# A fused linear attention and gated MLP on one core: a list scheduler that counts on longer hand-overs, and two quads of keys projected in plain float32

## The chip, the core and the metric

The kernel runs on one core of a Trainium2 chip. The core has TensorE (PE: matmuls, 128 x 128, results in PSUM), VectorE (DVE), ScalarE (ACT), GpSimd (POOL) and SyncE (SP), which here only issues DMAs. Each engine works through its own queue strictly in order and waits where an input is not there. The metric is the device time of one execution in microseconds, as a median over runs.

## The reference

Two stages. First linear attention over 8 batches x 8 heads, 576 positions, head dimension 64, with 128 features:

```python
def phi(x):
    proj = np.einsum('bhsd,df->bhsf', x, w_phi)
    proj = proj - np.max(np.abs(proj), axis=-1, keepdims=True)
    return np.concatenate([np.exp(proj), np.exp(-proj)], axis=-1)
q_p, k_p = (phi(q), phi(k))
kv = np.einsum('bhsf,bhsd->bhfd', k_p, v)
z = np.sum(k_p, axis=2)
num = np.einsum('bhsf,bhfd->bhsd', q_p, kv)
den = np.einsum('bhsf,bhf->bhs', q_p, z)[..., None] + 1e-06
return (num / den).astype(np.float32)
```

Then, with the heads side by side as `x` (576 x 512 per batch), a gated MLP with 1024 hidden columns:

```python
h = np.maximum(x @ w_in, 0.0)
# conv_out: each column of h filtered along the sequence with 3 taps, conv_w
gate = 1.0 / (1.0 + np.exp(-conv_out))
return (h * gate @ w_out).astype(np.float32)
```

`w_in`, `conv_w` and `w_out` come as float64, the rest as float32.

## The kernel before

**Number formats.** Most matmuls are done in three passes of a faster float32 format (F32R): an operand is split into a rounded part (`hi`) and the rest (`lo`), and hi x hi, hi x lo and lo x hi are summed in PSUM. The rounding is one instruction (`round_op`, line 264, 267 or 270 by engine), the rest another (`rest_op`, line 276). Plain float32 operands (F32) need no split; the matmul is then one instruction, which the profile records as two.

**Attention.** Heads are taken four at a time, a *quad*; there are 16, two per batch. A quad's 576 positions are cut into five groups, one of 128 columns (g = 0) and four of 256. The names in the trace carry batch, quad and group: `kp3_1_2` is the key projection of batch 3, quad 1, group 2. For a key group (`k_group`): DMA into `kr`; POOL splits it into `kxh` (line 267) and `kxl` (276); TensorE projects it to `kp` in PSUM (lines 409 to 411); VectorE takes the maximum `km` (420) and subtracts it, `ks` (423); ScalarE makes two exponentials `ke` (443); TensorE multiplies them with the values into `kv` (452, 456). For a query group (`q_group`), one quad later: `qr`, `qxh`, `qxl`, `qp`, `qm`, `qs` in the same way, then TensorE transposes `qs` into `tp` (506), ScalarE makes `qe` (521) and rounds it to `qh` (264), VectorE makes the rest `ql` (276), and TensorE multiplies with `kv` into `nm` (539, 546). The queries of the first two quads (`NQ_F32`) are projected in F32 from `qr` directly (line 406). Numerators are copied to `num` (587), denominators to `dr` (580) and by DMA to `den`; VectorE inverts them (`rc`), four DMAs spread them into the single buffer `rr`, and the matmul `rb` (613) copies them over the partitions; VectorE multiplies to `xf` (616), which is split into `xh` and `xl`.

**MLP.** Each batch has two halves of 288 columns, n = 0 to 15. For each, eight blocks f: `hp` (640) is x times `w_in`, 12 matmuls; ScalarE's Relu gives `h` (651); POOL makes the middle tap of `c` (664), VectorE adds two taps (670). One sigmoid over all of `c` (675) follows, with ScalarE's function table changed before and after; then `c` times `h` (683), split into `gh` (264) and `gl` (276), and `op` (704) times `w_out` into `os` (712), which a DMA stores.

**Weights.** The 16 blocks of `w_in` and `w_out` are brought from float64 to hi and lo on the chip during the first 200 us: four VectorE, three ScalarE and two POOL instructions each (lines 314 to 329, `w_t`).

**What sets the order.** All instructions are collected as ops (`op`) with an engine, a planned duration, a rank (urgency) and their inputs. `Order.run` is a list scheduler: it walks through planned time and, on each free engine, takes the ready op of lowest rank. An op is ready when its inputs have ended in the plan and the hand-over between the engines (`LATENCY`, less `OVERLAP` on VectorE and ScalarE) has passed, and when its buffers' earlier users have ended and their `LATENCY` has passed. The plan's times are used for nothing else: what it leaves is the order on each engine. On the chip the queues run that order, each instruction waiting for its real inputs.

Of the kernel before, what the change touches and what calls it, by code (L numbers as in the profile page):

```python
# [23 lines left out]
NH = 11  # L24

NQ_F32 = 2
NKV_F32 = 2
LAG = 3.0

PE, DVE, ACT, POOL, SP = "PE", "DVE", "ACT", "POOL", "SP"  # L30


class Buf:
# [4 lines left out]
    def __init__(self, pool, shape, dtype, name, tag, bufs, seq=None):  # L38


        self.args = (pool, shape, dtype, name, tag, bufs)
        Buf.count += 1
        self.seq = Buf.count if seq is None else seq
        self.ring = (id(pool), tag)
        self.bufs = bufs
        self.ops = []
        self.state = {}
        self.tile = None
# [16 lines left out]
class Order:  # L65
# [1 line left out]

    LATENCY = {PE: 250, DVE: 180, ACT: 180, POOL: 150, SP: 0}  # L70
    OVERLAP = {PE: 0, DVE: 60, ACT: 60, POOL: 0}
    TABLE_NS = 1283

    def __init__(self):
        self.ops = []
# [43 lines left out]
    def run(self):  # L119
        free = {e: 0.0 for e in (PE, DVE, ACT, POOL, SP)}  # L120
        waiting = {e: [] for e in free}
        rings, alloced = {}, set()
        line = {}
        for b in {b for o in self.ops for b in o.bufs}:
            if b.seq != "any":
                line.setdefault(b.ring, []).append(b)
        for bs in line.values():
            bs.sort(key=lambda b: b.seq, reverse=True)
        table, dma = None, 0.0
        for o in self.ops:  # L130
            o.left, o.at = len(o.deps), 0.0
            o.end = None
            if not o.left:
                waiting[o.eng].append(o)
        done, now, order = 0, 0.0, []
        while done < len(self.ops):
            best = None
            nxt = []
            for e, ws in waiting.items():
                if free[e] > now:  # L140
                    nxt.append(free[e])
                    continue
                pick = None
                for o in ws:
                    if o.at > now:
                        nxt.append(o.at)
                        continue
                    if pick is not None and pick.rank <= o.rank:
                        continue
                    ok = True  # L150
                    for b in o.bufs:
                        if b in alloced:
                            continue
                        if b.seq != "any" and line[b.ring][-1] is not b:
                            ok = False
                            break
                        ring = rings.setdefault(b.ring, [])
                        if len(ring) >= b.bufs:
                            old = ring[-b.bufs].ops
                            if any(x.end is None for x in old):  # L160
                                ok = False
                                break
                            t = max(x.end + self.LATENCY[x.eng] for x in old)
                            if t > now:
                                nxt.append(t)
                                ok = False
                                break
                    if ok:
                        pick = o
                if pick is not None:  # L170
                    best = pick
                    break
            if best is None:
                nxt = [t for t in nxt if t > now]
                if not nxt:
                    raise RuntimeError("no order: " + ", ".join(
                        f"{o.eng} {[b.args[3] for b in o.bufs]}" for ws in waiting.values() for o in ws)[:1500])
                now = min(nxt)
                continue
            o = best  # L180
            waiting[o.eng].remove(o)
            for b in o.bufs:
                if b not in alloced:
                    alloced.add(b)
                    rings[b.ring].append(b)
                    if b.seq != "any":
                        line[b.ring].pop()
            o.start = now
            ns = o.ns
            if o.table is not None and o.table != table:  # L190
                ns += self.TABLE_NS
                table = o.table
            if o.eng == SP:

                free[SP] = now + 60
                dma = max(dma, now) + ns
                o.end = dma + 2000
            else:
                o.end = now + ns
                free[o.eng] = o.end - self.OVERLAP[o.eng]  # L200
            for u in o.users:
                u.left -= 1
                u.at = max(u.at, o.end + (0 if u.eng == o.eng != SP else self.LATENCY[o.eng] - self.OVERLAP.get(o.eng, 0)))
                if not u.left:
                    waiting[u.eng].append(u)
            order.append(o)
            done += 1
        return order
# [3 lines left out]
def kernel(  # L212
# [119 lines left out]
    def weight_split(src, n, rank, hi, lo, hi_b, lo_b):  # L332

        name = f"w{n}_"
        if src.dtype == F32:
            raw = sbuf([P, 512], F32, f"{name}r", "gh", 2)
            dma(rank - 2, 256, lambda: raw.t, lambda: src, w=[raw])
            round_op(POOL, rank, 512, hi, lambda: raw.t, [(hi_b, n)], [raw])
            rest_op(POOL, rank, 512, lo, lambda: raw.t, hi, [(lo_b, n)], [raw, (hi_b, n)])
            return  # L340
        raw = sbuf([P, 1024], I32, f"{name}r", "gh", 2)
        dma(rank - 2, 512, lambda: raw.t, lambda: src, w=[raw])
        tmp = sbuf([P, 2, 512], F32, f"{name}t", "gl", 2)
        float64_round(rank, 512, lambda: raw.t, lambda: tmp[:, 0, :], lambda: tmp[:, 1, :],
                      raw, (tmp, 0), (tmp, 1))
        round_op(ACT, rank, 512, hi, lambda: tmp[:, 0, :], [(hi_b, n)], [(tmp, 0)])
        rest_op(POOL, rank, 512, lo, lambda: tmp[:, 0, :], hi, [(lo_b, n)], [(tmp, 0), (hi_b, n)])
# [16 lines left out]
    def load_weight(n, rank):  # L364
        if n < 8:
            c, sl = n // 2, slice((n % 2) * 512, (n % 2) * 512 + 512)
            weight_split(w_in[n], n, rank, lambda: win_hi[c][:, sl], lambda: win_lo[c][:, sl], win_hi[c], win_lo[c])
        else:
            c = n - 8
            weight_split(w_out[c], n, rank, lambda: wout_hi[c].t, lambda: wout_lo[c].t, wout_hi[c], wout_lo[c])  # L370
# [5 lines left out]
    def group_columns(g):  # L376
        return (512, 1) if g == 0 else ((g - 1) * 256 + (P if g > 2 else 0), 2)

    def load_split(src, b, qd, g, kind, rank):
        c0, n = group_columns(g)  # L380
        ap = lambda: src[b, qd, :, c0 : c0 + n * P]
        if kind == "q" and 2 * b + qd < NQ_F32:
            raw = sbuf([P, n * P], F32, f"{kind}r{b}_{qd}_{g}", kind + "xh", 2)
            dma(rank - 3, 64 * n, lambda: raw.t, ap, w=[raw])
            return n, raw, None
        raw = sbuf([P, n * P], F32, f"{kind}r{b}_{qd}_{g}", kind + "r", 2)
        dma(rank - 3, 64 * n, lambda: raw.t, ap, w=[raw])
        hi = sbuf([P, n * P], F32R, f"{kind}xh{b}_{qd}_{g}", kind + "xh", 2)
        lo = sbuf([P, n * P], F32R, f"{kind}xl{b}_{qd}_{g}", kind + "xl", 2)
        round_op(POOL, rank, n * P, lambda: hi.t, lambda: raw.t, [hi], [raw])  # L390
        rest_op(POOL, rank, n * P, lambda: lo.t, lambda: raw.t, lambda: hi.t, [lo], [raw, hi])
        return n, hi, lo
# [75 lines left out]
    def kv_ready(u):  # L468
# [4 lines left out]
        for i in range(2):  # L473
            kf = None
            if u >= NKV_F32:
                kf = sbuf([P, 2, 2 * VW], F32, f"kvf{b}_{qd}_{i}", "kvf", 2)
            hi = sbuf([P, 2, 2 * VW], F32 if u < NKV_F32 else F32R, f"kvh{b}_{qd}_{i}", "kvh", 4)
            first = hi if kf is None else kf
# [15 lines left out]
    def q_group(j):  # L494
# [13 lines left out]
        op(PE, 110 * 2 * n, rank, turn, w=[tp], r=[pr, idn])  # L508
        f32 = u < NKV_F32 or g == 0
        qh = sbuf([P, 2, 2, n * P], F32 if f32 else F32R, f"qh{b}_{qd}_{g}", "qh", 2)  # L510
# [111 lines left out]
    def moe_rank(n):  # L622
        return 10.0 + LAG + 5.0 * n

# [89 lines left out]


    for n in range(16):
        load_weight(n, 1 + 0.9 * n)
    hs = {}
    for j in range(5 * NQ * B + 5):
        if j < 5 * NQ * B:  # L720
            k_group(j)
        if j >= 5:
# [3 lines left out]
            if (j - 5) % 10 == 9:  # L726
                b = (j - 5) // 10
# [66 lines left out]
```

## Time and profile before

| | |
|---|---|
| median of 3 runs | 930.44 us (924.73 to 931.77) |
| profiled execution | 931.45 us, of which its instructions span 929.7 us |
| granted TensorE clock in it, mean | 0.972 |
| TensorE busy in the first 200 us | 156.1 us |
| MLP block hp, first | at 121.8 us |
| last stretch, op of the last half batch | 900.7 to 926.3 us |

The profile names work by line, engine and tile. A wait is put down to the instruction whose end came last before the waiting one started. A matmul's record is longer than its share of a stream, since matmuls are pipelined: the next one starts before the record of the one ahead ends. The granted clock is the share of full speed that TensorE was given in a stretch.

### The profile page before, as it was taken

What the parts mean: (1) busy time and instruction counts of PE and PEld (TensorE: products, weight loads), DVE (VectorE), ACT (ScalarE), POOL (GpSimd) and SP (SyncE); (2) the same over time, 40 slices, a digit from 0 to 9 for tenths busy, and PEclk for the clock granted to TensorE, in tenths of its full rate; (3) what the DMA queues carried; (4) which work ended last, traced back from release to release, by engine and by line L of the source; (5) the groups of instructions that cost most, each with busy time, mean ns of one, the idle gap of its engine ahead of it and who ended that gap; (6) DMA issues with size and microseconds to landing.
All of it is one profiled execution on the core that took longest, in us unless ns stands there. A gap on an engine that the chain in (4) does not pass through costs nothing.

```text
span 929.7 us, 17861 instructions
## 1 busy us (share of the span) xinstructions
PE 820.5 (88%) x6414; PEld 789.4 (85%) x6414; DVE 640.9 (69%) x1294; ACT 573.1 (62%) x1230; POOL 305.7 (33%) x469
## 2 busy tenths in 40 slices
PE   6977589789999889988999879998899989998998
PEld 5866588689998879988899879998789988998998
DVE  5666888887668676767776667686776677675652
ACT  4575666667666576666766646576666647574432
POOL 4553656441423223332322313242142323211110
PEclk9797989899999999999999999999999999999999
DMA  6343331121111111111211111121112110000001
GB/s 191 114 121 89 94 96 36 30 54 55 42 48 54 43 44 46 55 35 45 59 43 49 41 44 45 41 60 33 52 48 60 36 42 25 20 20 21 21 15 50
DMA packets 56336, 49.19 MB, mean 53 GB/s; under 512 B 15028, under 2 KB 54200, under 8 KB 56248
## 3 DMA queue, kind: packets, MB, share of 16 engines
q1 hardware_dynamic: 56248, 48.05, 17.9%
q8 instruction: 51, 0.84, 0.4%
q14 instruction: 37, 0.30, 0.1%
HBM read 38.14 MB, written 9.44 MB: 51 GB/s over the span
## 4 chain that ended last, share of the span: by engine, by line
PE 43%; DVE 20%; ACT 13%; issue 10%; DMA 4%; POOL 2%; SPq 1%; POOLq 0%; ACTq 0%; DVEq 0%
PE op L704 12%; PE hp L640 8%; PE nm L546 6%; PE kv L456 6%; DMA rr<-rc 3%; DVE c L670 3%; PE tp L506 3%; DVE ql L276 3%; ACT qh L264 3%; PE nm L539 2%; ACT num L587 2%; DVE gl L276 2%; DVE ks L423 2%; PE kv L452 2%; ACT ke L443 2%
## 5 line engine op out<-in xcount | busy, mean ns | idle before, releaser
L670 DVE SCALAR_TENSOR_TENSOR c<-h,cw,c 128x288 f32<-128x288 f32 (+1 forms) x256 | 143.4, 572 | 46.9 <-POOL c L664 43.8
L640 PE MATMUL hp<-xh,win_hi 128*128 128x290 f32 x512 | 154.7, 302 | 9.3 <-ACT h L651 7.0
L456 PEld LDWEIGHTS kv<-v,ke 128*128 128x128 f32 x1024 | 156.8, 198 | 6.6 <-ACT ke L443 2.3
L456 PE MATMUL kv<-v,ke 128*128 128x65 f32 x1024 | 160.0, 257 | 2.0 <-ACT ke L443 1.9
L640 PE MATMUL hp<-xl,win_hi 128*128 128x290 f32 x512 | 153.3, 300 | 0.4 <-DVE xl L276 0.4
L640 PE MATMUL hp<-xh,win_lo 128*128 128x290 f32 x512 | 152.8, 298 | 0.0
L704 PE MATMUL op<-gh,wout_hi 128*128 128x288 f32 x512 | 152.1, 297 | 0.0
L704 PE MATMUL op<-gl,wout_hi 128*128 128x288 f32 x512 | 150.8, 295 | 0.0
L704 PE MATMUL op<-gh,wout_lo 128*128 128x288 f32 x512 | 150.6, 294 | 0.0
L664 POOL TENSOR_SCALAR c<-h,cw 128x288 f32<-128x288 f32 x128 | 76.2, 597 | 215.7 <-ACT h L651 185.2
L443 ACT ACTIVATE ke<-ks 128x512 f32<-128x512 f32 (+1 forms) x160 | 87.1, 580 | 66.7 <-DVE ks L423 66.1
L276 DVE TENSOR_TENSOR ql<-qe,qh 128x512 fp32r<-128x512 f32 x112 | 84.0, 760 | 64.0 <-ACT qh L264 63.3
L587 ACT ACTIVATE num<-nm 64x256 f32<-64x256 f32 (+1 forms) x192 | 61.8, 322 | 99.6 <-PE nm L546 54.9
L267 POOL TENSOR_SCALAR kxh<-kr 128x256 fp32r<-128x256 f32 (+1 forms) x80 | 39.7, 496 | 250.8 <-PE kp L410 240.4
L640 PEld LDWEIGHTS hp<-xh,win_hi 128*128 128x128 f32 x512 | 98.5, 192 | 12.5 <-ACT h L651 8.3
L640 PEld LDWEIGHTS hp<-xl,win_hi 128*128 128x128 f32 x512 | 98.1, 192 | 0.6 <-DVE xl L276 0.6
L640 PEld LDWEIGHTS hp<-xh,win_lo 128*128 128x128 f32 x512 | 98.5, 192 | 0.0
L506 PE MATMUL tp<-idn,qs 128*128 128x128 f32 x288 | 48.2, 287 | 55.7 <-DVE qs L423 38.1
L704 PEld LDWEIGHTS op<-gh,wout_hi 128*128 128x128 f32 x512 | 96.4, 188 | 0.0
L704 PEld LDWEIGHTS op<-gh,wout_lo 128*128 128x128 f32 x512 | 96.4, 188 | 0.0
L704 PEld LDWEIGHTS op<-gl,wout_hi 128*128 128x128 f32 x512 | 96.4, 188 | 0.0
L506 PEld LDWEIGHTS tp<-idn,qs 128*128 128x128 f32 x288 | 32.7, 145 | 67.1 <-issue 31.4
(86 smaller groups left out, 2002.4 us busy)
## 6 DMA issues: line engine op xcount, KB each, us to landing
v<-in_vt_dram SPq DMA_DIRECT2D x80, 130.0 KB
out_dram<-os SPq DMA_DIRECT2D x64, 144.0 KB
kr<-in_kT_dram SPq DMA_DIRECT2D x64, 128.0 KB
qr<-in_qT_dram SPq DMA_DIRECT2D x64, 128.0 KB
w_r<-in_w_in_dram SPq DMA_DIRECT2D x8, 512.0 KB
w_r<-in_w_out_dram SPq DMA_DIRECT2D x8, 512.0 KB
rr<-rc SPq DMA_DIRECT2D x128, 2.2 KB
kr<-in_kT_dram SPq DMA_DIRECT2D x16, 64.0 KB
```

The source lines that it names most:

```text
L264: op(ACT, t_act(n), rank, lambda: nc.scalar.activation(out=hi(), in_=src(), func=AF.Copy), w=w, r=r)
L267: lambda: nc.gpsimd.tensor_scalar(out=hi(), in0=src(), scalar1=1.0, scalar2=0.0, op0=ALU.mult, op1=ALU.add),
L276: lambda: e.tensor_tensor(out=lo(), in0=src(), in1=hi().bitcast(F32), op=ALU.subtract), w=w, r=r)
L443: op(ACT, t_act(256 * n), rank, lambda s=s: nc.scalar.activation(out=e[:, s], in_=pr.t, func=AF.Exp, scale=1.0 - 2.0 * s), w=[(e, s)], r=[ ...
L456: nc.tensor.matmul(out=kp[i][:, s, p0 : p0 + VW], lhsT=lhsT, rhs=v[:, (2 * t + i) * VW : (2 * t + i + 1) * VW], start=False, stop=(g % 2 = ...
L506: nc.tensor.transpose(out=tp[:, i, t, :], in_=pr[:, 2 * t + i, :], identity=idn.t)
L546: nc.tensor.matmul(out=ps[:, i, o : o + w], lhsT=w_, rhs=x_, start=(k == 0), stop=(k == 5))
L587: op(ACT, 170 + 0.82 * w, rank, lambda i=i, o=o, w=w, s0=s0, nt=nt: nc.scalar.activation(out=nt[D * i : D * i + D, s0 : s0 + w], in_=ps[0: ...
L640: nc.tensor.matmul(out=ps.t, lhsT=w_, rhs=x_, start=(p == 0 and k == 0), stop=(p == 3 and k == 2))
L664: op(POOL, 620, rank, lambda f=f, hs=hs: nc.gpsimd.tensor_scalar(out=c4[:, f, :], in0=hs[:, o : o + TC], scalar1=cw3[:, f, 1:2], scalar2=0 ...
L670: op(DVE, 550, rank, lambda f=f, hs=hs, j=j, lo=lo, hi=hi: nc.vector.scalar_tensor_tensor(out=c4[:, f, lo:hi], in0=hs[:, o + j - 1 + lo : ...
L704: nc.tensor.matmul(out=ps.t, lhsT=w_, rhs=x_, start=(f == 0 and k == 0), stop=(f == 7 and k == 2))
```

## The change

Three things. The planner's hand-over times grow: from TensorE 250 to 560 ns, from VectorE and ScalarE 180 to 420, from POOL 150 to 400; the same numbers delay the reuse of buffers. A new table `SLACK` adds to each hand-over between two engines, for ops of rank above 0, 400 ns where the waiting engine is TensorE and 100 ns where it is VectorE, ScalarE or POOL. And the keys of the first two quads (`NK_F32`, batch 0) are projected in F32: no `kxh` and `kxl` on POOL for those ten groups, one F32 matmul per tile in place of three. Their raw tiles then use the buffers of `kxh`. The two names for the weights' ranks keep their values.

```diff
+NK_F32 = 2
+W_RANK, W_STEP = 1.0, 0.9
...
-    LATENCY = {PE: 250, DVE: 180, ACT: 180, POOL: 150, SP: 0}
+    LATENCY = {PE: 560, DVE: 420, ACT: 420, POOL: 400, SP: 0}
     OVERLAP = {PE: 0, DVE: 60, ACT: 60, POOL: 0}
     TABLE_NS = 1283
+
+    SLACK = {PE: 400, DVE: 100, ACT: 100, POOL: 100, SP: 0}
...
-                u.at = max(u.at, o.end + (0 if u.eng == o.eng != SP else self.LATENCY[o.eng] - self.OVERLAP.get(o.eng, 0)))
+                gap = 0 if u.eng == o.eng != SP else self.LATENCY[o.eng] - self.OVERLAP.get(o.eng, 0)
+                if u.eng != o.eng and u.rank > 0:
+                    gap += self.SLACK[u.eng]
+                u.at = max(u.at, o.end + gap)
...
-        if kind == "q" and 2 * b + qd < NQ_F32:
+        if 2 * b + qd < (NQ_F32 if kind == "q" else NK_F32):
...
-        load_weight(n, 1 + 0.9 * n)
+        load_weight(n, W_RANK + W_STEP * n)
```

The order changes on every engine. Line numbers of the changed kernel are 7 higher from the planner's loop on. The numbers at the end of names count buffers.

VectorE at the query group of batch 3, quad 0, group 1, from its maximum `qm` on, before:

```order
L420 TENSOR_REDUCE qm3_0_1_4049<-qp3_0_1_3896 128x4
L616 TENSOR_TENSOR xf2_3_0_4059<-num2_1_1_3339,rb2_3_0_4047 128x290
L616 TENSOR_TENSOR xf2_3_1_4067<-num2_1_1_3339,rb2_3_1_4051 128x290
L423 TENSOR_TENSOR ks3_1_1_4071<-kp3_1_1_3886,km3_1_1_4044 128x512
L276 TENSOR_TENSOR xl2_3_0_4083<-xf2_3_0_4059,xh2_3_0_4069 128x290
L276 TENSOR_TENSOR gl3_0_4086<-c3_3471,gh3_0_4073 128x288
L276 TENSOR_TENSOR xl2_3_1_4093<-xf2_3_1_4067,xh2_3_1_4081 128x290
L276 TENSOR_TENSOR gl3_0_4086<-c3_3471,gh3_0_4073 128x288 x3
L276 TENSOR_TENSOR gl3_4_4124<-c3_3471,gh3_4_4107 128x288 x4
L423 TENSOR_TENSOR qs3_0_1_4133<-qp3_0_1_3896,qm3_0_1_4049 128x512
```

and after:

```order
L427 TENSOR_REDUCE qm3_0_1_3985<-qp3_0_1_3818 128x4
L283 TENSOR_TENSOR xl2_2_0_3991<-xf2_2_0_3948,xh2_2_0_3973 128x290
L283 TENSOR_TENSOR xl2_2_1_3999<-xf2_2_1_3970,xh2_2_1_3987 128x290
L430 TENSOR_TENSOR qs3_0_1_4003<-qp3_0_1_3818,qm3_0_1_3985 128x512
L427 TENSOR_REDUCE km3_1_2_4015<-kp3_1_2_3950 128x4
```

The subtraction `qs`, for which TensorE's `tp` waits, stands ahead of the eight `gl` and not behind them.

VectorE where the second quad's first group comes, batch 3, quad 1, group 0, with one step of the convolution `c`, before:

```order
L420 TENSOR_REDUCE km4_0_0_4549<-kp4_0_0_4529 128x2
L420 TENSOR_REDUCE qm3_1_0_4552<-qp3_1_0_4535 128x2
L423 TENSOR_TENSOR ks4_0_0_4560<-kp4_0_0_4529,km4_0_0_4549 128x256
L670 SCALAR_TENSOR_TENSOR c4_4163<-h4_6_4533,cw_77,c4_4163 128x287
L423 TENSOR_TENSOR qs3_1_0_4578<-qp3_1_0_4535,qm3_1_0_4552 128x256
```

and after:

```order
L427 TENSOR_REDUCE km4_0_0_4473<-kp4_0_0_4451 128x2
L427 TENSOR_REDUCE qm3_1_0_4475<-qp3_1_0_4456 128x2
L430 TENSOR_TENSOR ks4_0_0_4485<-kp4_0_0_4451,km4_0_0_4473 128x256
L430 TENSOR_TENSOR qs3_1_0_4488<-qp3_1_0_4456,qm3_1_0_4475 128x256
L677 SCALAR_TENSOR_TENSOR c4_4160<-h4_6_4468,cw_77,c4_4160 128x287
```

`c` moved behind `qs`.

TensorE in the first 200 us, from the projection `qp0_1_0` to its transposes `tp0_1_0`, before:

```order
L406 MATMUL qp0_1_0_658<-wbd_f_70,qr0_1_0_514 128x256
L409 MATMUL kp1_0_1_666<-wbd_hi_71,kxh1_0_1_603 128x256
L410 MATMUL kp1_0_1_666<-wbd_lo_72,kxh1_0_1_603 128x256
L411 MATMUL kp1_0_1_666<-wbd_hi_71,kxl1_0_1_608 128x256
L409 MATMUL kp1_0_1_666<-wbd_hi_71,kxh1_0_1_603 128x256
L410 MATMUL kp1_0_1_666<-wbd_lo_72,kxh1_0_1_603 128x256
L411 MATMUL kp1_0_1_666<-wbd_hi_71,kxl1_0_1_608 128x256
L506 MATMUL tp0_1_0_703<-idn_73,qs0_1_0_696 128x128 x2
```

and after, the last rows before the transposes (`qp0_1_0` itself stands 16 rows ahead of them):

```order
L418 MATMUL kp1_0_1_557<-wbd_hi_71,kxl1_0_1_503 128x256
L546 MATMUL nm0_0_3_568<-qh0_0_3_496,kvh0_0_0_318 65x256
L463 MATMUL kv0_1_0_373<-v0_1_3_320,ke0_1_3_461 128x65 x2
L546 MATMUL nm0_0_3_568<-qh0_0_3_496,kvh0_0_0_318 65x256
L463 MATMUL kv0_1_1_378<-v0_1_3_320,ke0_1_3_461 128x65 x2
L546 MATMUL nm0_0_3_568<-qh0_0_3_496,kvh0_0_1_324 65x256
L463 MATMUL kv0_1_0_373<-v0_1_3_320,ke0_1_3_461 128x65 x2
L546 MATMUL nm0_0_3_568<-qh0_0_3_496,kvh0_0_1_324 65x256
L463 MATMUL kv0_1_1_378<-v0_1_3_320,ke0_1_3_461 128x65 x2
L513 MATMUL tp0_1_0_599<-idn_73,qs0_1_0_566 128x128 x2
```

A whole group of `nm` with its share of `kv`, and a transpose of the group before (further up), moved in between `qp` and `tp`.

## The prediction

> **What bounds the kernel now.** I read the page's totals first, then TensorE's waits in two windows (the first 200 us and the rest), then single places in the timeline, then the table of stretches for the granted clock.
>
> ```profile
> PE 820.5 (88%) x6414; PEld 789.4 (85%) x6414; DVE 640.9 (69%) x1294; ACT 573.1 (62%) x1230; POOL 305.7 (33%) x469
> ```
>
> TensorE is the busiest engine. It has 12% idle, and no other engine is near full over the whole span. So what can be won without less work is TensorE's idle time, and the question is who ends it. First 200 us, then the rest (each row: who waited for whom, total us, times, longest):
>
> ```profile
> PE tp L506 <- DVE qs L423: 13.2, 8, 3.3
> PE hp L640 <- ACT h L651: 7.0, 2, 6.0
> PE tp L506 <- ACT w_t L316: 6.6, 1, 6.6
> PE kp L409 <- POOL kxh L267: 6.1, 4, 3.6
> ```
>
> ```profile
> PE tp L506 <- DVE qs L423: 24.9, 25, 1.8
> PE rb L613 <- DMA rr<-rc: 18.4, 14, 2.0
> PE tp L506 <- ACT ke L443: 8.2, 10, 1.2
> ```
>
> One place in the program dominates both: tp, the transposes of the projected queries, which need the subtraction qs on VectorE. After 200 us tp waits 24.9 + 8.2 = 33.1 us in 35 waits, 0.95 us each. That is a hand-over TensorE to VectorE and back inside one group: qp (TensorE), qm and qs (VectorE), tp (TensorE). The next row, rb waiting for the DMAs into rr, is a different chain.
>
> Is it the hand-over itself that is long, or VectorE's queue? Two waits of the steady part, in time order. First tp of the group (3,0,1):
>
> ```profile
> 329.38 3.41 DVE L276 TENSOR_TENSOR gl<-c,gh 128x288 fp32r<-128x288 f32 x7
> 332.71 0.68 DVE L423 TENSOR_TENSOR qs<-qp,qm 128x512 f32<-128x512 f32 x1
> ```
>
> ```profile
> 333.44 0.66 PE L506 MATMUL tp<-idn,qs 128*128 128x128 f32 x4 [1.72 <-DVE qs L423]
> ```
>
> qs ends at 333.39 and tp starts at 333.44: the hand-over takes 0.05 us. What came late is qs, which stands behind seven gl in VectorE's queue. Second, tp of (3,1,0):
>
> ```profile
> 362.11 0.28 PE L411 MATMUL qp<-wbd_hi,qxl 128*128 128x256 f32 x1
> 363.56 0.41 DVE L420 TENSOR_REDUCE km<-kp 128x2 f32<-128x256 f32 x1
> 364.55 1.05 DVE L670 SCALAR_TENSOR_TENSOR c<-h,cw,c 128x287 f32<-128x287 f32 x1
> 365.53 0.41 DVE L423 TENSOR_TENSOR qs<-qp,qm 128x256 f32<-128x256 f32 x1
> 366.08 0.41 PE L506 MATMUL tp<-idn,qs 128*128 128x128 f32 x2 [1.17 <-DVE qs L423]
> ```
>
> The last qp ends at 362.39, qs at 365.94. VectorE gets to the group's km 1.17 us after qp's end, and a convolution step c (1.05 us here) stands between. So the planner's old 0.12 us from VectorE to TensorE is about what the chip takes; the loss is that nothing is left over when VectorE runs late. The change gives just such a reserve.
>
> **The change part by part.** *Longer hand-overs and slack, steady part.* The planner now lets tp start 0.76 us after qs (0.12 before) and qm 0.66 us after qp (0.25 before). It does not slow the chip; it moves other TensorE work in between. I counted the TensorE work that stands in the order between a group's last qp and its tp. It costs this much per matmul of 288 columns (54 of them in 7.18 us, 0.133 each):
>
> ```profile
> 264.13 7.18 PE op L704 x54
> ```
>
> With 0.12 us for each kp and qp, the work in one batch (batch 3, the same in 4 to 6) is, before and after: first quad, groups 0 to 4: 2.6 to 3.8 us, 12.7 to 11.8, 3.1 to 7.4, 2.4 to 3.1, 2.4 to 4.0; second quad: 2.6 to 2.6, 7.2 to 8.7, 7.9 to 3.1, 1.9 to 4.1, 2.4 to 5.5. The seven classes that have 3.1 us or less before are those that wait, with (3,0,1). Six of the seven gain 0.7 to 4.3 us, against a mean wait of 0.95. The seventh, (b,1,0), gains no work, but the c of 1.05 us no longer stands between its ks and qs. The class (b,0,1) loses 0.9 us of work, but its qs now stands ahead of all eight gl, of which the seven above took 3.41 us. The class (b,1,2) falls to 3.1 us; VectorE needs 0.68 us each for qm and qs there, behind four gl, so it can wait up to about 1 us where it did not.
>
> What stays: 0.1 to 0.6 us in six or seven (b,1,0), 3.6 at most, and 1.5 for the newly short class; 5 in all. Bounds: everything goes (33.1) or, if VectorE's lateness grows with the reserve, nothing. I take 28 because in each class the added work is larger than the wait seen.
>
> *rb and rr.* Late next is this chain:
>
> ```profile
> 431.20 3.09 SPq L246 DMA_DIRECT2D rr<-rc  x4
> ...
> 435.51 0.51 PE L613 MATMUL rb<-rr,sel_r 128*128 128x290 f32 x2 [1.22 <-DMA rr<-rc]
> ```
>
> rr has one buffer. Its four DMAs are issued as soon as the pair of rb before has read it (SyncE needs 3.09 us for them), and the next rb starts 435.51 - 431.20 = 4.3 us after the first issue. In the order 24 op (3.2 us) stand between two pairs before; after, 24 op for one and 24 op with 6 kp (3.9 us) for the next. That saves 0.7 once a batch. But the pair ahead of them was covered by a tp wait that goes, and has 3.9 us of work against 4.3. I take 0 of the 18.4, with -5 to +8 as bounds (plus 8: twenty pairs at 1.3 each are 26).
>
> *The first 200 us.* Here tp has almost no cover: in the first four quads several tp stand 0.4 to 0.9 us behind their qp. One of them, (0,1,0):
>
> ```profile
> 60.18 0.65 PE L406 MATMUL qp<-wbd_f,qr 128*128 128x256 f32 x2
> ...
> 60.79 0.28 PE L410 MATMUL kp<-wbd_lo,kxh 128*128 128x256 f32 x1
> ...
> 62.93 0.41 PE L506 MATMUL tp<-idn,qs 128*128 128x128 f32 x2 [1.40 <-DVE qs L423]
> ```
>
> In the second quad the cover grows from 0.7, 0.9, 2.9, 0.9, 0.4 us to 4.0, 3.5, 4.8, 6.8, 3.9. tp waits 13.2 + 6.6 = 19.8 us here. But VectorE is nearly full once the weights and batch 1 run together (the stretch from 110 to 200 us below: 77.31 of 90), and what it has to do there is not less. So I take 14 of the 19.8: all that lies before 110 us but the 6.6, which ends on the weights' chain, and little after. Bounds 0 and 19.8.
>
> *The f32 keys.* POOL loses two instructions in each of ten groups:
>
> ```profile
> L276 POOL TENSOR_TENSOR kxl<-kr,kxh 128x256 fp32r<-128x256 f32 (+1 forms) x80 | 61.9, 774 | 5.7
> ...
> L267 POOL TENSOR_SCALAR kxh<-kr 128x256 fp32r<-128x256 f32 (+1 forms) x80 | 39.7, 496 | 250.8 <-PE kp L410 240.4 <-PE kv L456 5.4 <-DMA kr<-in_kT_dram 4.8
> ```
>
> That is 10 x (0.77 + 0.50) = 12.7 us of an engine that is a third busy. On the path only the wait kp <- kxh counts, 6.1 us with 3.6 of it the start of the program, when the data still lands. I take 2 (bounds 0 and 6.1). TensorE pays: from the start of the qp above to the second kp is 0.61 us, less 0.12 for the first kp is 0.49 for one f32 tile, against 3 x 0.12 = 0.36. That is +0.13 for 18 tiles, +2.3 us; bounds 0.2 (0.65 less a tail of 0.28) and 5.2 (0.65 without that deduction). The start lists keys of batch 1 ahead of a group of batch 0 in SyncE's queue, 0.2 MB more before it; it is inside the 2.
>
> *The granted clock.* Waits cost twice in the first part, as it seems:
>
> ```profile
> 34.00:40.00 6.00, 5.97 (x37) 5.51 (x36) 5.50 (x10) 2.43 (x6) 3.83 (x6) 0.68 0.27 80
> 50.00:60.00 10.00, 6.73 (x39) 5.75 (x37) 6.53 (x13) 5.38 (x11) 6.57 (x7) 0.83 0.32 94
> 80.00:90.00 10.00, 5.61 (x22) 4.81 (x23) 6.71 (x12) 4.72 (x10) 4.38 (x6) 0.61 0.41 115
> 110.00:120.00 10.00, 4.45 (x27) 4.42 (x28) 9.03 (x19) 4.46 (x9) 3.68 (x4) 0.66 0.25 80
> 110.00:200.00 90.00, 72.01 (x540) 68.74 (x541) 77.31 (x142) 57.72 (x123) 47.94 (x60) 0.91 0.19 54
> ```
>
> (Columns: TensorE, its weight loads, VectorE, ScalarE, POOL busy with counts, granted clock, DMA.) In the stretches that hold the long waits the clock is 0.83, 0.61 and 0.66; the share lost of the busy time is 6.73 x 0.17 + 5.61 x 0.39 + 4.45 x 0.34 = 4.8 us. If the low clock follows the waits, these go too; I leave them out of the sum and in the lower bound. The Trainium skill ("TensorE: Matmul & The Clock Gate", Part 1) says the clock halves after an idle window of about 3.4 us and is released after about 3.4 us of sustained work. By that rule only the waits of 6.6 us and 6.0 us would throttle, and the sum stays as it is; by the rows, where a longest wait of 3.3 us is followed by low clock, it would be 4.8 us lower. The row from 34 to 40 us speaks against the release too: TensorE is busy 5.97 of 6 us at 0.68.
>
> **Sum**, on the profiled execution (931.45 us, span 929.7): 931.45 - 28 - 0 - 14 - 2 + 2.3 = 889.8. That execution lies 1.0 above the median of the runs, so 889 against 930.44.
>
> **The rivals.**
> *Half of it turns into other waits.* TensorE reaches rb and nm earlier and waits there. For: rr's chain is a fixed 4.3 us; and the cover between tp and its nm in the second quad falls from 12.4 to 8.4 (group 1) and 9.8 to 6.7 us (group 4). Against: nm waits for nearly nothing now. Price: rb +7.6 (26 less 18.4), nm 1 us in seven batches, half the prologue's 14: 889 + 7.6 + 7 + 7 = 911.
> *The change does not do what it says.* VectorE's lateness (POOL ahead of c, contention) grows as the order moves, so the waits stay and only the f32 keys count, about 0: 931. For: the 0.05 us hand-over above was never the loss. Against: the added cover is TensorE work, whatever made VectorE late.
> *Slower: SyncE's queue.* Output DMAs wait for os on ScalarE and stand between the rr DMAs; os can be held by the sigmoid with a table load on each side.
>
> ```profile
> L675 ACT ACTIVATE c<-c 128x2304 f32<-128x2304 f32 x16 | 34.1, 2130 | 4.2 <-DVE c L670 4.0
> ...
> L675 ACT ACT_TABLE_LOAD x14 | 18.0, 1283 | 0.2
> ...
> SPq L246 <- ACT os L712: 72.5, 27, 15.9
> ```
>
> If an rr issue falls behind that block in each of 16 half batches, TensorE waits 16 x (2.13 + 2 x 1.28) = 75 us at rb and the gain of 42 turns into a loss: 931 - 42 + 75 - 2 = 962. It decides from 42 / 16 = 2.6 us per half batch. For: SyncE waits 72.5 us for os already. Against: rb waits only 18.4 in all after 200 us today, and the same two output DMAs stand there in both orders.
>
> **How the numbers follow.** 0.60 for the forecast (its own range 866 to 905), 0.21 for half of it (905 to 921), 0.11 for no effect, 0.08 for slower. The lower end: 889 less the 5 of tp left, the 5.8 left in the prologue, 4.8 of clock, 2.1 of the f32 bound and 5 of rb's, 866. The upper end: 911 and 2.9 (f32), 2 (POOL) and 7 (the rest of the prologue) more, 923. It leaves out the last two cases, 0.19. About 1% (9.3 us) is what a measurement of this kernel can tell from no change: faster 0.81, same 0.11, slower 0.08.
>
> **What would show it.** Right: after 200 us the waits of tp fall from 33 to under 8 and rb stays at 15 to 22; in the first 200 us tp falls from 20 to some 6, and the clock in 50 to 120 us rises; TensorE's busy share rises to about 92%. The f32 step shows as kp at the f32 line with no POOL row ahead of it. Wrong: rb or nm at the top of TensorE's waits with 25 us or more; a tp wait that still ends on qs in most groups; or VectorE at over 95% from 110 us on with the prologue as long as before.

## The result, and the profile after

| | before | after |
|---|---|---|
| median | 931.11 us (924.73 to 931.81, 4 runs) | 866.84 us (865.63 to 868.32, 4 runs) |
| ratio, 95% interval | 1 | 0.9325 [0.9281, 0.9369] |
| profiled execution, its span | 931.45, 929.7 us | 868.32, 866.5 us |
| first hp of half batch 4 | 330.0 us | 310.7 us |
| first hp of half batch 12, four batches later | 768.2 us | 713.2 us |
| one batch between these two | 109.6 us | 100.6 us |

The kernel is 64 us (6.7%) faster, where 42 was forecast. The starts of `hp` are read off the timeline by the order of the instructions. They divide the gain: 19.3 us before half batch 4, 35.7 us in four whole batches, 8.2 us after them.

The page's totals after:

```profile
PE 807.2 (93%) x6396; PEld 785.1 (91%) x6396; DVE 635.5 (73%) x1294; ACT 571.7 (66%) x1230; POOL 302.4 (35%) x449
```

TensorE's busy share went from 88 to 93%. Its waits in the first 200 us after (us, times, longest):

```profile
PE kp L413 <- DMA kr<-in_kT_dram: 7.1, 4, 3.2
PE kp L416 <- DVE ks L430: 6.3, 3, 5.0
PE nm L553 <- ACT num L594: 3.7, 1, 3.7
...
PE tp L513 <- DVE qs L430: 1.6, 2, 1.1
```

and after 200 us (two more rows, of 0.5 and 0.2 us, complete the list):

```profile
PE rb L620 <- DMA rr<-rc: 17.0, 17, 2.2
PE nm L546 <- ACT num L594: 3.4, 11, 0.3
PE op L711 <- ACT os L719: 2.3, 5, 0.5
...
PE tp L513 <- DVE xf L623: 0.3, 1, 0.3
```

In the later window `tp` is down to 0.3 us from 34; `rb` hardly moved. In the early one `tp` is small too, but `kp` now waits on a DMA and on the subtraction `ks`.

The place that the prediction looked at, group (3,1,0), in the timeline after:

```profile
335.25 0.28 PE L418 MATMUL qp<-wbd_hi,qxl 128*128 128x256 f32 x1
...
336.59 0.42 DVE L430 TENSOR_TENSOR qs<-qp,qm 128x256 f32<-128x256 f32 x1
...
337.05 0.99 DVE L677 SCALAR_TENSOR_TENSOR c<-h,cw,c 128x287 f32<-128x287 f32 x1
...
337.76 0.30 PE L711 MATMUL op<-gh,wout_lo 128*128 128x288 f32 x1
...
337.89 0.38 PE L513 MATMUL tp<-idn,qs 128*128 128x128 f32 x2
```

`qs` ends at 337.01, and `tp` starts at 337.89, 0.13 us behind the `op` ahead of it: no wait, and 0.88 us to spare. Before, it started 0.14 us after `qs`.

Three stretches that the prediction used for the clock, after (TensorE, weight loads, VectorE, ScalarE, POOL, granted clock):

```profile
50.00:60.00 10.00, 9.72 (x69) 8.38 (x69) 8.91 (x18) 8.59 (x18) 6.63 (x7) 1.00 0.47 138
80.00:90.00 10.00, 9.37 (x59) 8.02 (x59) 7.00 (x14) 6.03 (x13) 6.05 (x7) 0.83 0.36 105
110.00:120.00 10.00, 8.48 (x70) 8.03 (x70) 8.27 (x11) 8.54 (x18) 5.93 (x6) 0.96 0.37 108
```

Before, the clock in them was 0.83, 0.61 and 0.66. The same stretches hold other work now, but TensorE waits less in them and is slowed less.

### The profile page after: what moved, and what is told of

Read it like the earlier page. It is cut to its first block, busy times and chain, and to the rows that moved or that the text cites. A ratio compares the mean times of both kernels' runs of the same rounds, so it can differ in the third digit from the quotient of the medians.

```text
span 866.5 us, 17785 instructions
## 1 busy us (share of the span) xinstructions
PE 807.2 (93%) x6396; PEld 785.1 (91%) x6396; DVE 635.5 (73%) x1294; ACT 571.7 (66%) x1230; POOL 302.4 (35%) x449
## 5 line engine op out<-in xcount | busy, mean ns | idle before, releaser
L677 DVE SCALAR_TENSOR_TENSOR c<-h,cw,c 128x288 f32<-128x288 f32 (+1 forms) x256 | 146.6, 581 | 29.9 <-POOL c L671 27.3
L671 POOL TENSOR_SCALAR c<-h,cw 128x288 f32<-128x288 f32 x128 | 78.0, 611 | 179.0 <-ACT h L658 173.5
L283 DVE TENSOR_TENSOR ql<-qe,qh 128x512 fp32r<-128x512 f32 x112 | 77.4, 710 | 36.6 <-ACT qh L271 36.5
L274 POOL TENSOR_SCALAR kxh<-kr 128x256 fp32r<-128x256 f32 (+1 forms) x70 | 31.3, 446 | 204.7 <-PE kp L417 196.5
L450 ACT ACTIVATE ke<-ks 128x512 f32<-128x512 f32 (+1 forms) x160 | 89.6, 582 | 18.5 <-DVE ks L430 17.4
L658 ACT ACTIVATE h<-hp 128x290 f32<-128x290 f32 x128 | 51.4, 408 | 65.4 <-PE hp L647 53.8
L427 DVE TENSOR_REDUCE km<-kp 128x4 f32<-128x512 f32 (+1 forms) x80 | 50.5, 631 | 50.9 <-PE kp L418 38.0
```

The lines of the kernel that those rows point to most:

```text
L274: lambda: nc.gpsimd.tensor_scalar(out=hi(), in0=src(), scalar1=1.0, scalar2=0.0, op0=ALU.mult, op1=ALU.add),
L283: lambda: e.tensor_tensor(out=lo(), in0=src(), in1=hi().bitcast(F32), op=ALU.subtract), w=w, r=r)
L427: op(DVE, t_dve(256 * n) - 40, rank, lambda: nc.vector.tensor_reduce(out=m.t, in_=ps.t.rearrange("p (t f) -> p t f", f=F), axis=AX, op=ALU ...
L450: op(ACT, t_act(256 * n), rank, lambda s=s: nc.scalar.activation(out=e[:, s], in_=pr.t, func=AF.Exp, scale=1.0 - 2.0 * s), w=[(e, s)], r=[ ...
L658: op(ACT, 412, rank - 0.5, lambda hs=hs, ps=ps: nc.scalar.activation(out=hs.t, in_=ps.t, func=AF.Relu), w=[hs], r=[ps])
L671: op(POOL, 620, rank, lambda f=f, hs=hs: nc.gpsimd.tensor_scalar(out=c4[:, f, :], in0=hs[:, o : o + TC], scalar1=cw3[:, f, 1:2], scalar2=0 ...
```

## The experiments

Medians, with the ratio to the kernel before run on the same chip, and the time of one batch between the two `hp` above:

| kernel | us | ratio [95%] | one batch, us |
|---|---|---|---|
| float32 keys alone | 933.55 | 1.003 [1.0007, 1.0053] | 109.3 |
| buffer hand-back alone | 919.37 | 0.9884 [0.9856, 0.9913] | 107.5 |
| slack alone (and keys) | 913.48 | 0.9812 [0.9786, 0.9837] | 107.4 |
| reserve ahead of tp alone | 903.21 | 0.9699 [0.9664, 0.9735] | 106.2 |
| that and the hand-back | 897.09 | 0.9647 [0.9611, 0.9683] | 103.8 |
| half of the numbers (and keys) | 891.31 | 0.9591 [0.9543, 0.9638] | 105.6 |
| all but the hand-back | 886.83 | 0.9547 [0.9500, 0.9594] | 104.2 |
| all but the slack | 876.92 | 0.9407 [0.9368, 0.9446] | 102.4 |
| the whole change | 866.84 | 0.9325 [0.9281, 0.9369] | 100.6 |
| order alone, no keys | 864.49 | 0.9287 [0.9268, 0.9306] | 100.8 |
| two sets of rr rows | 864.27 | 0.9283 [0.9253, 0.9313] | 101.2 |
| these two together | 864.07 | 0.9300 [0.9258, 0.9343] | 101.2 |
| double the numbers (and keys) | 845.52 | 0.9088 [0.9054, 0.9122] | 97.7 |

**The two parts apart.** The first kernel takes the float32 keys with the old planner:

```diff
-    LATENCY = {PE: 560, DVE: 420, ACT: 420, POOL: 400, SP: 0}
+    LATENCY = {PE: 250, DVE: 180, ACT: 180, POOL: 150, SP: 0}
-    SLACK = {PE: 400, DVE: 100, ACT: 100, POOL: 100, SP: 0}
+    SLACK = {PE: 0, DVE: 0, ACT: 0, POOL: 0, SP: 0}
```

> The planner's numbers as before, only the keys of the first two quads in plain float32. Theory (the reserve in the hand-overs brings the gain): 926 to 934 us, and tp still waits about 33 us after 200 us and about 20 us in the first 200. Rival (the keys bring the gain of 16 us that the first 195 us show): 912 to 918 us, with tp's waits in the first 200 us down.

The second takes the new planner without the keys:

```diff
-NK_F32 = 2
+NK_F32 = 0
```

> The new hand-overs and slack, keys of the first two quads in three passes as before. Theory: 864 to 874 us, nearly all of the gain, tp's waits after 200 us under 3 us. Rival (the keys bring the first 16 us): 880 us or more, with the loss in the first 195 us.

The keys alone give 933.55 us, 0.3% slower, and the order alone 864.49, as fast as the whole change. The gain is all the planner's. Two rows of TensorE's waits with the keys alone, in the first 200 us:

```profile
PE tp L513 <- DVE qs L430: 15.6, 8, 6.4
...
PE kp L413 <- DMA kr<-in_kT_dram: 4.9, 3, 3.2
```

The wait of `kp` for POOL's `kxh` (6.1 us before) has gone, and one on the keys' own DMA has come in its place.

**Hand-over times or slack.** Without the slack:

```diff
-    SLACK = {PE: 400, DVE: 100, ACT: 100, POOL: 100, SP: 0}
+    SLACK = {PE: 0, DVE: 0, ACT: 0, POOL: 0, SP: 0}
```

> The new hand-over times, slack at zero, float32 keys kept. From qp to tp the plan then has 0.55 us more than before, against 1.05 with the slack. Theory (the reserve counts, in proportion): 885 to 905 us, tp waits 8 to 20 us after 200 us. Rival (what counts is that buffers are reused later, which this keeps whole): 866 to 872 us.

and with the slack but the old hand-over times:

```diff
-    LATENCY = {PE: 560, DVE: 420, ACT: 420, POOL: 400, SP: 0}
+    LATENCY = {PE: 250, DVE: 180, ACT: 180, POOL: 150, SP: 0}
```

> The slack with the old hand-over times, float32 keys kept. From qp to tp the plan has 0.50 us more than before. Theory (the reserve counts, in proportion): 885 to 905 us, about as the run with the hand-over times alone. Rival (later reuse of buffers counts, which this lacks): 922 to 932 us.

876.92 and 913.48 us: each lies between its two theories, so that neither holds; the second was expected about as fast as the first and is not. With the slack alone the waits of `tp` after 200 us have gone, and still only 1.9% is won. Its list after 200 us begins:

```profile
PE rb L620 <- DMA rr<-rc: 18.7, 15, 2.1
PE qp L416 <- DVE qs L430: 9.1, 5, 2.7
PE hp L647 <- ACT os L719: 6.0, 5, 1.8
PE kp L416 <- DVE ks L430: 3.4, 7, 1.0
```

`qp` and `kp` need no result of `qs` and `ks`. They wait for the PSUM buffer that those read last. This hand-back is counted with `LATENCY` alone; the slack does not reach it. The granted clock takes a part too: in the four batches of the slack alone it is halved six times for 3.4 us (0.50 from 329.8 to 333.2 us, for one), which loses 2.6 us a batch; before, it is halved once, for 6.8 us, which loses 0.9.

**Only the reserve ahead of tp.** In the kernel before, the planner holds `tp` 640 ns longer and changes nothing else:

```diff
-                u.at = max(u.at, o.end + (0 if u.eng == o.eng != SP else self.LATENCY[o.eng] - self.OVERLAP.get(o.eng, 0)))
+                u.at = max(u.at, o.end + (0 if u.eng == o.eng != SP else self.LATENCY[o.eng] - self.OVERLAP.get(o.eng, 0) + u.reserve))
...
-        op(PE, 110 * 2 * n, rank, turn, w=[tp], r=[pr, idn])
+        op(PE, 110 * 2 * n, rank, turn, w=[tp], r=[pr, idn]).reserve = 640
```

> The planner as before, only tp has to stand 0.64 us later after its qs in the plan (0.76 in all, as in the change); nothing else. Theory A (the wait of tp is the loss; any reserve in front of it brings the time): 880 to 895 us. Theory B (a reserve at one place moves the wait to the next hand-over, as the run with the slack alone showed for qp and kp, which wait for qs and ks to free their PSUM buffer): tp waits under 10 us, but 905 to 928 us with new waits of qp, kp or hp of 10 us or more.

903.21 us, between the two theories. It took almost all of the wait on which the prediction's sum rests; its list after 200 us begins:

```profile
PE rb L614 <- DMA rr<-rc: 23.0, 15, 2.8
PE hp L641 <- ACT os L713: 7.3, 7, 1.3
PE kp L410 <- DVE ks L424: 5.2, 5, 1.0
...
PE tp L507 <- DVE qs L424: 0.7, 3, 0.3
```

The wait of `tp` for `qs` and `ke` fell from 33.1 us to 0.7. But `rb` rose from 18.4 us to 23.0, `hp` waits 7.3 us for a PSUM buffer that `os` gives back, and `kp` 5.2 for one from `ks`, for which it did not wait before.

**Only the buffers' hand-back.** The new numbers where a buffer's reuse is counted, and nowhere else, in the kernel before:

```diff
+    REUSE = {PE: 560, DVE: 420, ACT: 420, POOL: 400, SP: 0}
...
-                            t = max(x.end + self.LATENCY[x.eng] for x in old)
+                            t = max(x.end + self.REUSE[x.eng] for x in old)
```

> The planner as before, only the reuse of a buffer is counted with the longer times (from TensorE 560 ns, VectorE and ScalarE 420, POOL 400). Theory A (hand-overs of data are what counts): 925 to 935 us, tp's waits as before. Theory B (both are needed, the hand-back alone does little for tp): 910 to 932 us with tp's waits at 20 us or more after 200 us. If the hand-back alone were the cause: 866 to 880 us.

The reverse, the changed kernel with the same line and `REUSE = {PE: 250, DVE: 180, ACT: 180, POOL: 150, SP: 0}`:

> The changed kernel, but the planner counts the reuse of a buffer with the times of before (from TensorE 250 ns, VectorE and ScalarE 180, POOL 150); hand-overs and slack stay new. Theory A (hand-overs of data are what counts): 864 to 872 us. Theory B (the hand-back of buffers is a hand-over like the others and needs the reserve too): 880 to 912 us, with waits of qp and kp on qs and ks of 8 us or more after 200 us.

And the reserve ahead of `tp` together with the first `REUSE`:

> The kernel before with the two single parts together: a reserve of 640 ns ahead of the transposes only, and the buffers' hand-back counted at the new times; all other hand-overs as before, no float32 keys. Alone they took 28.0 us and 11.8 us off. Theory A (they take off different waits and add): 931.2 - 39.8 = 891, that is 887 to 896. Theory B (each moves its wait to the place that the other frees, so together more than the sum): 866 to 885, near the whole order (864.5). Theory C (the same waits counted twice): 897 to 905.

The hand-back alone takes off 11.8 us, and leaving it out of the change costs 20: more where the hand-overs around it are covered. Both times are in theory B's ranges; the waits that it named are not what came. With the hand-back alone the waits of `tp` after 200 us are 16.0 us, where 20 or more were named. With the hand-back left out, `qp` and `kp` do not wait for `qs` and `ks` at all after 200 us, where 8 us or more were named; instead `hp` waits 5.9 us for `xl` and 2.8 for `h`, and `tp` 4.0 for `qs`, 30.2 us of all waits against 23.7 in the change. So the times show that the hand-back's numbers count, and not that the cost is at `qp` and `kp`. With the reserve ahead of `tp` the hand-back gives 897.09 us, at the edge of theory C (897 to 905) and 1 us above theory A's range: 33.6 us off, where the two alone add up to 39.8. Each interval is some 3 us to either side, so that this does not safely part the two. It does speak against theory B, and it leaves 30 us of the change to hand-overs that are neither of the two.

**Half and double.** `LATENCY` 405/300/300/275 with `SLACK` 200/50/50/50, and 870/660/660/650 with 800/200/200/200:

> The changed kernel with half of the step from old to new reserves: hand-over times 405/300/300/275 in place of 560/420/420/400, slack 200/50/50/50 in place of 400/100/100/100; float32 keys kept. Theory A (the gain grows with the reserve, since each ns of it takes as much off the waits): half way between the float32 keys alone (933.6) and the whole change (866.8), that is 890 to 910. Theory B (a reserve only has to pass the real delay of a hand-over, and most of the waits in the steady part are then gone at once): 862 to 880, with tensor waits on the transposes of queries under 5 us after 200 us.

> The changed kernel with the step from old to new reserves doubled: hand-over times 870/660/660/650, slack 800/200/200/200; float32 keys kept. Theory A (more reserve, fewer waits): the 24 us of shown waits that are left after 200 us, most of them of rb on the row's transfer, shrink to about half: 850 to 860. Theory B (past the real delays a reserve buys nothing in the steady part, and in the first 200 us it holds ready work back): 866 to 885. Theory C (the longer leads need more buffers than there are, so that the planner leaves holes on the tensor engine): over 885.

891.31 us lies in theory A's range; 845.52 lies below all three ranges of the double, on theory A's side. From the keys alone (933.6) the time falls by 42 us for the first half of the step, 24 for the second and 21 for as much again as the whole. Theory A's reason, that each ns takes as much off the waits, is not what the half shows: its waits of `tp` after 200 us are down to 1.0 us, as theory B had it, but `qp` waits 10.9 us for the PSUM buffer that `qs` gives back, and half speed loses it 1.7 us a batch. The longest of the double's waits after 200 us in sum:

```profile
PE rb L620 <- DMA rr<-rc: 7.8, 10, 3.2
```

The stretch from 200 to 600 us of before, after and double:

```profile
200.00:600.00 400.00, 363.72 (x2975) 354.15 (x2974) 281.76 (x580) 259.24 (x554) 121.98 (x202) 0.99 0.17 47
```

```profile
200.00:600.00 400.00, 385.75 (x3222) 381.11 (x3222) 296.58 (x616) 277.68 (x602) 136.10 (x224) 1.00 0.18 50
```

```profile
200.00:600.00 400.00, 393.89 (x3309) 391.37 (x3308) 311.09 (x643) 284.44 (x622) 133.21 (x231) 1.00 0.19 52
```

In the same 400 us TensorE does 2975, 3222 and 3309 matmuls and is busy 91, 96 and 98.5%. By this share little is left to win there by order alone. Where a still larger reserve begins to cost was not tried.

**The wait that was left.** `rb` waits for the single `rr`. Here `rr` alternates between rows 0 to 3 and rows 32 to 35, so that the next four DMAs need not wait for the pair of `rb` before; `rb` then sums over these 4 rows in place of 128. The second kernel does this without the float32 keys:

```diff
+                k = 32 * (p % 2) + 2 * j + i
...
-                    w=[(rr, (i, j))], r=[rhl[j]])
+                    w=[(rr, (p % 2, i, j))], r=[rhl[j]])
+        k0 = 32 * (p % 2)
...
-                out=rb.t, lhsT=sel_r.t, rhs=rr[:, t0 : t0 + HW], start=True, stop=True), w=[rb], r=[sel_r, rr],
+                out=rb.t, lhsT=sel_r[k0 : k0 + 4, :], rhs=rr[k0 : k0 + 4, t0 : t0 + HW], start=True, stop=True), w=[rb],
+               r=[sel_r] + [(rr, (p % 2, i, j)) for i in range(2) for j in range(2)],
```

> The changed kernel with two sets of rows for rr (rows 0 to 3 and 32 to 35 of the same tile, by turns), so that the four DMAs into rr no longer wait for the rb before; rb contracts 4 rows and not 128. Theory (rb waits because rr has one buffer and its four issues take 3.1 us): rb's waits after 200 us fall from 17 us to under 5, and the time by 12 to 18 us, to 849 to 856 us. Rival (the waits go to what follows, xf and hp, or the DMAs come late for another reason): 862 to 868 us.

> The order alone (no float32 keys) together with two sets of rows for rr. Theory A (the two savings are of different waits and add up): 866.8 - 2.4 (float32 keys) - 2.6 (two sets of rows) = 861.9, that is 860 to 863.5. Theory B (one hides the other: another plan, the same end): 864 to 867.

864.27 and 864.07 us: the first is in its rival's range, the second in its theory B's, and neither can be told from the order alone, nor from the change. Yet the wait itself went, from 17.0 to

```profile
PE rb L623 <- DMA rr<-rc: 5.8, 11, 1.1
```

What it gave was lost at the same instructions. In the timeline, an `rb` of the change that waits for nothing, and one of the first of these two kernels:

```profile
336.83 0.29 PE L647 MATMUL hp<-xh,win_lo 128*128 128x290 f32 x1
336.96 0.30 PE L620 MATMUL rb<-rr,sel_r 128*128 128x290 f32 x1
337.10 0.29 PE L711 MATMUL op<-gh,wout_hi 128*128 128x288 f32 x1
337.23 0.29 PE L711 MATMUL op<-gl,wout_hi 128*128 128x288 f32 x1
```

```profile
329.80 0.29 PE L651 MATMUL hp<-xh,win_lo 128*128 128x290 f32 x1
330.02 0.40 PE L623 MATMUL rb<-rr,sel_r 4*128 4x290 f32 x1
330.35 0.40 PE L715 MATMUL op<-gh,wout_hi 128*128 128x288 f32 x1
330.58 0.29 PE L715 MATMUL op<-gl,wout_hi 128*128 128x288 f32 x1
```

From the `hp` ahead to the second `op` behind it took 0.40 us, and now takes 0.78. Over the 32 `rb` of the four batches, from the start of the matmul ahead to the start of the second one behind, waits included, it was 24.8 us and is 26.2; a batch became about half a microsecond longer. Whether a second whole buffer for `rr`, with `rb` still over 128 rows, would have kept the gain was not tried.

## Why the prediction was right, and where it was not

- **What bounds it**: right. TensorE's idle time was what could be won; the busy share of 92% that was named came out at 93.
- **Steady tp waits, 28 us**: the step that was mis-sized. The waits went more fully than forecast (from 33.1 us to 0.3, for another input; 5 were to stay). The class (b,1,2), feared to wait about 1 us, does not wait, nor does (b,1,0). But the sum booked the reserve at `tp` alone, on shown idle, and the gain of four batches is 35.7 us, where 28 of 730 us makes 17. Three things were missing. First, the reserve works at every hand-over and at every buffer's return. With it at `tp` alone a batch gains 3.3 us, with all of it 8.9; the waits move on to `kp`, `hp` and `rb` unless those are covered too. Second, a shown wait is shorter than the time it costs: a record of a matmul lasts 0.30 us and its share of a stream is 0.13, so about 0.17 of each wait lies under the record ahead. The class (b,0,3), which the prediction counted among those that wait, shows that part alone: in batches 2 to 7 it has no wait of over 0.03 us, and yet its `tp` starts 0.28 to 0.32 us after the matmul ahead. Third, the clock, which the prediction looked at in the first part only.

The waits from 330 to 660 us, three batches, account for the second point. Before:

```profile
PE tp L506 <- DVE qs L423: 13.9, 13, 1.8
PE rb L613 <- DMA rr<-rc: 8.1, 6, 2.0
PE tp L506 <- ACT ke L443: 4.9, 6, 1.2
PE nm L539 <- ACT dr L580: 3.6, 6, 0.6
PE hp L640 <- ACT os L712: 0.8, 3, 0.3
PE tp L506 <- DVE rc L598: 0.6, 1, 0.6
```

and after:

```profile
PE rb L620 <- DMA rr<-rc: 7.2, 8, 1.2
PE nm L546 <- ACT num L594: 2.1, 7, 0.3
PE op L711 <- ACT os L719: 2.1, 4, 0.5
PE rb L620 <- DVE gl L283: 0.5, 1, 0.5
```

That is 31.9 us in 35 waits against 11.9 in 20; in a batch 31.9 x 109.6 / 330 = 10.6 us and 11.6 waits against 3.6 us and 6.1 waits. The shown part gives 7.0, the hidden part 5.5 x 0.17 = 0.9, together 7.9 of the 8.9 us. Half speed makes most of the rest: in the four batches before, the granted clock is 0.50 from 553.2 to 560.0 us, 3.4 us lost or 0.9 a batch; in those after it is never lowered.

- **rb, 0 of 18.4 us**: right, 17.0 with 15 to 22 named. That `rb` would take over what `tp` gave up is what the reserve at `tp` alone shows (23.0), not the change.
- **First 200 us, 14 us**: the direction held, the size is not settled. The wait of `tp` for `qs` fell from 13.2 us to 1.6, and the 6.6 for the weights went. The first `op` starts at 178.9 us in place of 194.6, 15.7 earlier, where the terms for this part came to 13.7. But that start is a rough mark: with the keys alone it came 6.6 us earlier and the span was 2 longer. Counted from half batch 4 back, of the 19.3 us won by then some 11 (135 us of steady work at 8.9 in 109.6) belong to the steady part, and 8 are left.
- **Float32 keys, -2 + 2.3 us**: small, as forecast, but on the cost side: +0.3% alone (interval 0.07 to 0.53%). The first `hp` of half batch 4 comes 2.7 us later with the keys than without them, under the old planner (332.7 against 330.0) and under the new (310.7 against 308.0). The step that failed is "2 for POOL": the data's DMA took the place of `kxh` (4.9 us with the keys alone, 7.1 in the change).
- **Clock, left out of the sum**: it rose from 50 to 120 us, as named. By the prediction's own working its three stretches lost 4.8 us and now lose 9.37 x 0.17 + 8.48 x 0.04 = 1.9. Of the rule of the Trainium skill ("TensorE: Matmul & The Clock Gate", Part 1), an idle window of about 3.4 us ahead of the low clock, the runs show otherwise; see the last section.
- **Rivals**: *half of it turns into other waits* is true of the reserve at `tp` alone (903) and of the slack alone (913), and not of the whole, since its hand-back and its other hand-overs cover the next places. *No effect* fell. *SyncE's queue* did not come: `rb` waits no longer than before.
- **Range**: the time, 866.84, stands at its lower end, 866, and that it is still inside is in part luck. Of the terms that make this end, the last 5 us of `tp` came, but `rb` gave 1.4 of its 5, and the keys cost time where 2.1 more were to be won. What filled the gap, the other hand-overs, the returns of buffers and the hidden part of the waits, was not in the sum.

## What to carry to other kernels

When a list scheduler leaves short waits at many places, reserve planned time at all hand-overs at once, the return of buffers among them: a reserve at the place that waits most hands a good part of the wait to the next. Look for the size by doubling until the time turns; here it had not turned at twice the change. Book a wait on a pipelined engine at its shown idle plus the part of the record ahead that would have been overlapped, and look for the waits that a step uncovers before its worth is set down.

## What the hardware showed that was not expected

Waits of about 2 us were followed by a low clock, and so were pairs of shorter ones close together. In the kernel with the reserve at `tp` alone, TensorE waits for `rr`, and shortly after runs at half speed:

```profile
416.61 0.51 PE L614 MATMUL rb<-rr,sel_r 128*128 128x290 f32 x2 [2.13 <-DMA rr<-rc]
416.96 0.29 PE L705 MATMUL op<-gh,wout_hi 128*128 128x288 f32 x1
417.09 0.29 PE L705 MATMUL op<-gl,wout_hi 128*128 128x288 f32 x1
...
417.40 0.44 PE L705 MATMUL op<-gh,wout_hi 128*128 128x288 f32 x1
417.64 0.44 PE L705 MATMUL op<-gl,wout_hi 128*128 128x288 f32 x1
```

The stretch up to its end, and the one behind it:

```profile
417.20:420.50 3.30, 3.30 (x16) 3.30 (x15) 3.30 (x8) 0.81 (x2) 0.00 (x0) 0.51 0.07 19
420.50:424.00 3.50, 3.50 (x28) 3.50 (x28) 1.68 (x4) 2.85 (x5) 0.00 (x0) 0.97 0.13 43
```

A matmul takes 0.24 us in place of 0.13, for 3.3 us, with TensorE busy throughout; 14 of them lose 1.5 us on top of the wait. In this run the four longest waits of `rb` after 200 us (2.13 to 2.76 us) are each followed by such a stretch, and those of 1.92 and less are not. Other runs draw no such line: some waits of 2.1 to 2.3 us went without, with the slack alone four waits of 1.82 to 1.90 us were followed by one, and with the old hand-back in the change each of three such stretches follows two waits that end 1.3 us apart, the first of 1.12 to 1.30 us and the second of 0.8. One of the three:

```profile
309.22 0.40 PE L648 MATMUL hp<-xl,win_hi 128*128 128x290 f32 x1 [1.26 <-DVE xl L284]
310.56 0.83 PE L514 MATMUL tp<-idn,qs 128*128 128x128 f32 x4 [0.81 <-DVE qs L431]
```

```profile
310.90:314.30 3.40, 3.40 (x20) 3.40 (x19) 1.15 (x3) 0.60 (x1) 0.00 (x0) 0.50 0.00 0
```

So the length of a single wait does not decide it; what does is not shown.

The Trainium skill ("TensorE: Matmul & The Clock Gate", Part 1) has about 3.4 us for both the idle window and the release: the release agrees with the 3.3 us here, the idle window does not, since a low clock followed waits of 1.8 us.

The other is the 4-row matmul above: it and the two behind it start 0.22, 0.33 and 0.23 us after the matmul ahead of each, where it is 0.13, 0.14 and 0.13 with a 128-row one of the same width. Why is not shown.
